# Linear attention feeding a two-layer network, on one core: tiles laid on 512-byte lines, w_in in three pieces, and a new order of one block's visits

## The chip, the core and the metric

The kernel runs on one core of one Trainium2 chip. The core has five engines that run side by side, each through its own list of instructions in order, and that wait for each other by semaphores: TensorE (PE, matmuls, with its weight loads shown as PEld), VectorE (DVE), ScalarE (ACT), GpSimd (POOL) and SyncE (SP, which here only issues transfers). Tiles lie in SBUF, 128 partitions wide; matmuls write to PSUM. Transfers from device memory are issued by SP, ACT or POOL and carried out by the core's 16 DMA engines. The metric is the time of one execution on the device in microseconds (us), the median over runs; lower is better.

## What is computed

q, k and v are fp32 of [4 batches, 8 heads, 768 positions, 64]. Each head keeps a state that decays, and its output is the input of a two-layer network with a leaky activation:

```python
gamma = 1.0 - 2.0 ** (-5.0 - np.arange(H, dtype=np.float32))
for t in range(S):
    state = gamma[None, :, None, None] * state + np.einsum('bhd,bhe->bhde', k[:, :, t], v[:, :, t])
    y[:, :, t] = scale * np.einsum('bhd,bhde->bhe', q[:, :, t], state)
...
x = np.ascontiguousarray(attn_out.transpose(0, 2, 1, 3)).reshape(B * S, H * D)
h = x @ w_in                                       # [3072, 512] @ [512, 2048]
g = np.maximum(h, 0.0) + alpha * np.minimum(h, 0.0)
return (g @ w_out).astype(np.float32)              # [3072, 2048] @ [2048, 512]
```

## The kernel before

**Tiling.** The 3072 tokens are 24 units of 128 positions, and six blocks of four units (512 tokens). Work on the attention goes by visits: visit i takes a pair of neighbouring units and half of the heads (four), so that block n has the visits 4n to 4n+3. The matmuls of the network go by blocks: `ffn1(n)` is 64 products of 128x512 (16 tiles of the 2048 hidden features, called ft, by four parts of the 512 inputs), `ffn2(n)` again 64 (four groups of 128 tokens by 16 ft).

**One visit.** `load` (L110) brings k, q and v of a visit, 256 KB each, as fp32, by SP. `u_scale(i, a)` (L128) multiplies k (a=0) or q (a=1) by powers of gamma and casts to f16, into the tile kdq; unless an engine is given, k goes to DVE and q to POOL. `u_cast` (L146) casts v to f16 (vx), on POOL or ACT. `u_turn` (L160) transposes kdq on PE (eight matmuls named trb), and ACT copies the result to SBUF (kq); later blocks use `u_flip`, a transposing transfer, instead. `u_state` (L183) sums k times v on PE (stp); the function that it returns, `advance`, adds this to the decayed state (DVE, ss, L218) and multiplies the sum with the next decay (POOL, tg, L219). At a sequence's first unit DVE does both at once (L214). `u_scores` (L225) multiplies q with k (sca, scb) and returns `masked`, with which DVE applies the mask (m, L249). `u_out` (L259) multiplies the scores with v and the queries with the decayed state (yps), and ACT copies that into xT, the network's input. `u_visit` (L533) is state, scores, decays and masks of one visit; `u_prep` (L540) is both scales and the cast.

**The network.** In `ffn1` each ft's product lands in a PSUM tile (hps); ACT takes relu(-h) (hm, L336) and DVE makes g from both (gt, L337). With early=4, the first four ft are computed on the block's first 256 tokens first, so that they can start before the second pair of units is out. In `ffn2` with parts=4 the 64 matmuls go in four groups of 16, each for four ft: the first 16 need the tiles 0 to 3 of w_out, the next 16 the tiles 4 to 7, and so on. ACT copies the results out (os).

**The order.** `manual_schedule` (L74) keeps the instructions of each engine in the order in which the kernel's lines name them. Both network functions are generators, and `tick(gen, m)` (L386) lets them emit m matmuls; between ticks the kernel names attention work of the next block. So in block 0's ffn2, the visits 4 to 7 of block 1 lie at stated distances. Since every engine goes in order, work named early on POOL stands ahead of work named later, whatever is ready.

**Weights.** w_in is fetched by POOL with a cast to f16 (`get_wi(lo, hi)`, L409, tiles lo to hi of 16), in four pieces of 2, 4, 4 and 6 tiles named among visits 1 to 3. `hold` (L415) lets the first load of w_out wait until the third piece (tiles 6 to 10) has landed. `load_wo(i)` (L426) fetches four tiles of w_out as fp32 by SP, in turn with the loads of visits 4 to 7, and `cast_wo` (L431) casts a tile to f16, on POOL or ACT. w_out's pieces and k, q, v share 24 buffers ("ld"). PSUM has eight tiles of 512 fp32, shared by everything ("ps", bufs=8). `keep(m)` (L97) is m matmuls on constant data.

**SBUF's layout.** The pools lay tiles one behind another. The first ones take per partition 208 bytes (tab), 768 (mi), 2048 (gmat), 512 (alpha), 1024 (spin), 4 (warm) and 64 (oma), each rounded up to 32 bytes, behind 16,512 bytes of other use; all that follow (w_in, w_out, the loads and the working tiles) take multiples of 512 and so begin 192 bytes past a multiple of 512.

Of the kernel before, what the change touches and what calls it, by code (L numbers as in the profile page):

```python
# [9 lines left out]
FP = mybir.dt.float32  # L10
F16 = mybir.dt.float16
# [7 lines left out]
def kernel(  # L19
# [13 lines left out]
    NFT = d_ff // 128  # L33
# [13 lines left out]
    NTAB = 4 * H + NP + 16  # L47
# [24 lines left out]
    sbp = ctx.enter_context(tc.tile_pool(name="sbp", bufs=1, space=bass.MemoryType.SB))  # L72
    psp = ctx.enter_context(tc.tile_pool(name="psp", bufs=1, space=bass.MemoryType.PSUM))
    ctx.enter_context(tc.manual_schedule())  # L74

    tab = sbp.tile([128, NTAB], FP, tag="tab", name="tab")
    mi = sbp.tile([128, 384], F16, tag="mi", name="mi")
    ident = mi[:, 0:128]
    masku = mi[:, 128:384].rearrange("p (s i) -> p s i", s=2)
    gmat = sbp.tile([128, NP, 128], FP, tag="gmat", name="gmat")  # L80
    alpha_sb = sbp.tile([NFT, 128], FP, tag="alpha", name="alpha")
    spin = sbp.tile([128, 512], F16, tag="spin", name="spin")
    warm = sbp.tile([128, 1], FP, tag="warm", name="warm")
    oma_sb = sbp.tile([128, NFT], FP, tag="oma", name="oma")
    w_in_all = sbp.tile([128, 4, d_ff], F16, tag="win", name="win")
    w_out_all = sbp.tile([128, NFT, d_model], F16, tag="wout", name="wout")

# [5 lines left out]
    def ps(name, dt=FP, n=512):  # L93
        return psp.tile([128, n], dt, tag="ps", bufs=8, name=name)


    def keep(m):  # L97
        pt = ps("kps")
        for i in range(m):
            nc.tensor.matmul(  # L100
                out=pt, lhsT=spin[:, 0:128], rhs=spin, start=True, stop=True
            )
# [5 lines left out]
    held = []  # L108
# [19 lines left out]
    def u_scale(i, a, eng=None):  # L128
        if i not in prepped:
            kdq = sbp.tile([128, 2, 2, H // 2, D], F16, tag="kdq", bufs=8, name=f"kdq{i}")  # L130
            kq = sbp.tile([128, 2 * NP, 128], F16, tag="kq", bufs=8, name=f"kq{i}")
            vx = sbp.tile([128, H // 2, 2, D], F16, tag="vx", bufs=8, name=f"vx{i}")
            prepped[i] = (kdq, kq, vx)
        g = i % 2
        o = 2 * H * a
        (eng or (nc.vector, nc.gpsimd)[a]).tensor_tensor(  # L136
            out=prepped[i][0][:, a],
            in0=staged[i]["kq"[a]].rearrange("p (h s d) -> p s h d", s=2, d=D),
            in1=tab[:, o : o + 2 * H]
            .rearrange("p (s h) -> p s h", s=2)[:, :, H // 2 * g : H // 2 * g + H // 2]  # L140
            .unsqueeze(3)
            .to_broadcast([128, 2, H // 2, D]),
            op=MULT,
        )

    def u_cast(i, on_scalar=False):  # L146
        o = prepped[i][2].rearrange("p h s d -> p (h s d)")
        x = staged[i]["v"]
        if on_scalar:
            nc.scalar.activation(out=o, in_=x, func=COPY, bias=0.0, scale=1.0)  # L150
        else:
            nc.gpsimd.tensor_copy(out=o, in_=x)  # L152
# [7 lines left out]
    def u_turn(i, parts):  # L160
        kdu, kq, vx = prepped[i]
        trb = ps("trb", F16, 1024)
        for a in parts:
            for x in range(NP):
                c0 = 128 * (NP * a + x)
                nc.tensor.transpose(  # L166
                    out=trb[:, c0 : c0 + 128],
                    in_=kdu[:, a, x // 2, 2 * (x % 2) : 2 * (x % 2) + 2, :].rearrange(
                        "p a d -> p (a d)"
                    ),  # L170
                    identity=ident,
                )
        c0 = 512 * parts[0]
        c1 = 512 * parts[-1] + 512
        nc.scalar.activation(  # L175
            out=kq.rearrange("p a i -> p (a i)")[:, c0:c1],
            in_=trb[:, c0:c1],
            func=COPY,
            bias=0.0,
            scale=1.0,  # L180
        )
# [77 lines left out]
    def u_out(i):  # L259
        j, g = divmod(i, 2)  # L260
        kqv, vx, m2s = live.pop(i)
        prepped.pop(i)
        ypss = [ps("yps"), ps("yps")]
        inter = [(2 * j + hf) % NCH > 0 for hf in range(2)]

        def carried(first):
            for hf in range(2):
                z = slice(64 * hf, 64 * hf + 64)
                for r in range(2):
                    if inter[hf]:  # L270
                        nc.tensor.matmul(  # L271
                            out=ypss[hf][:, 128 * r : 128 * r + 128],
                            lhsT=tgs[2 * j + hf][:, 2 * g + r, :],
                            rhs=kqv[:, 1, :, r, z],
                            start=(first and r == 0),
                            stop=(not first and r == 1),
                            skip_group_check=True,
                        )

        def own(first):  # L280
            for r in range(2):
                for s in range(2):
                    for lh in range(2):
                        for hf in range(2):
                            z = slice(64 * hf, 64 * hf + 64)
                            nc.tensor.matmul(  # L286
                                out=ypss[hf][64 * lh : 64 * lh + 64, 128 * r : 128 * r + 128],
                                lhsT=vx[z, 2 * r + lh, s, :],
                                rhs=m2s[lh][z, s, r, :],
                                start=(r == 0 and s == 0 and (first or not inter[hf])),  # L290
                                stop=(r == 1 and s == 1 and not (first and inter[hf])),
                                skip_group_check=True,
                            )

        if i < 2 * UB:
            own(True)
            carried(False)
        else:
            carried(True)
            own(False)  # L300
        n, jj = divmod(j, UB // 2)
        if n not in xT:
            xT[n] = sbp.tile([128, NP, TB], F16, tag="xT", bufs=2, name=f"xT{n}")
        for hf in range(2):
            c0 = C * (2 * jj + hf)
            nc.scalar.activation(  # L306
                out=xT[n][:, 2 * g : 2 * g + 2, c0 : c0 + C].rearrange(
                    "p a (i s) -> p a s i", s=2
                ),
                in_=ypss[hf][:, 0:256].rearrange("p (a s i) -> p a s i", a=2, s=2),  # L310
                func=COPY,
                bias=0.0,
                scale=1.0,
            )
# [71 lines left out]
    def tick(gen, m):  # L386
        for _ in range(m):
            if next(gen, 1) == 1:
                return
# [19 lines left out]
    def get_wi(lo, hi):  # L409
        s = slice(128 * lo, 128 * hi)  # L410
        return nc.gpsimd.dma_start(out=w_in_all[:, :, s], in_=wi[:, :, s])
# [19 lines left out]
    def cast_wo(ft, on_scalar=False):  # L431
        if on_scalar:
            nc.scalar.activation(
                out=w_out_all[:, ft, :], in_=pieces.pop(ft), func=COPY, bias=0.0, scale=1.0
            )
        else:
            nc.gpsimd.tensor_copy(out=w_out_all[:, ft, :], in_=pieces.pop(ft))  # L437

    m = {}
    st = {}  # L440
# [21 lines left out]
    st[0] = u_state(0)  # L462
    u_scale(2, 0)
    u_scale(2, 1)
    get_wi(0, 2)
    st[0](0)
    m[1] = u_scores(1)
    masked(1)
# [7 lines left out]
    st[1] = u_state(1)  # L476
    u_scale(3, 0)
    u_scale(3, 1)
    get_wi(2, 6)
    st[0](1)  # L480
    st[1](0)
    m[2] = u_scores(2)
    masked(2)
    keep(2)
    held.append(get_wi(6, 10))
    st[1](1)

    u_turn(3, (0, 1))
# [4 lines left out]
    st[2](0)  # L493
    get_wi(10, 16)
    m[3] = u_scores(3)
    keep(2)
    st[3] = u_state(3)
    m[3](0)
    st[3](0)
    m[3](1)  # L500
    for i in range(UB):
        load_wo(i)
        load(UB + i)
    gen = ffn1(0, early=4)
# [6 lines left out]
    nc.vector.tensor_scalar(  # L511
        out=oma_sb, in0=aps[:, 0:NFT], scalar1=-1.0, scalar2=1.0, op0=MULT, op1=ADD
    )
    st[2](1)
    st[3](1)
    for ft in range(4):
        cast_wo(ft)

    tick(gen, 8)
    u_out(3)  # L520
    tick(gen, 40)
    u_scale(4, 1)
    u_cast(4)
    for ft in range(4, 8):
        cast_wo(ft)
    tick(gen, 20)
    for _ in gen:
        pass
    u_scale(4, 0)
    stores = []  # L530
    gen = ffn2(0, parts=4, late=stores)

    def u_visit(i):  # L533
        st[i] = u_state(i)
        m[i] = u_scores(i)
        st[i](0)
        masked(i)
        st[i](1)

    def u_prep(i, eng=None):  # L540
        u_scale(i, 0, eng)
        u_scale(i, 1)
        u_cast(i)

    tick(gen, 6)
    u_turn(4, (0, 1))
    tick(gen, 6)
    u_visit(4)
    u_prep(5)
    tick(gen, 8)  # L550
    u_turn(5, (0, 1))
    tick(gen, 2)
    u_out(4)
    tick(gen, 4)
    u_visit(5)
    for ft in range(8, 12):
        cast_wo(ft, ft % 2)
    u_prep(6)
    tick(gen, 8)
    u_turn(6, (0, 1))  # L560
    tick(gen, 2)
    u_out(5)
    tick(gen, 4)
    u_visit(6)
    for ft in range(12, 16):
        cast_wo(ft, ft % 2)
    u_prep(7)
    tick(gen, 8)
    u_turn(7, (0, 1))
    tick(gen, 2)  # L570
    u_out(6)
    tick(gen, 4)
    u_visit(7)
    for _ in gen:
        pass
# [4 lines left out]
    gen = ffn1(1, early=4)  # L580
# [3 lines left out]
    for n in range(1, NBLK):  # L584
        more = n + 1 < NBLK
        u0 = UB * (n + 1)
        if n > 1:
            gen = ffn1(n)
# [9 lines left out]
        gen = ffn2(n)  # L598
# [41 lines left out]
```

## Time and profile before

| what | value |
|---|---|
| median of 3 runs | 224.21 us (224.03 to 225.7) |
| the profiled execution | 224.33 us, of which the profile's span is 222.5 us |
| granted TensorE clock in it | 0.997 |
| busy: PE, DVE, ACT, POOL | 208.7, 120.2, 102.7, 87.9 us |
| read from and written to device memory | 27.40 MB and 6.29 MB |
| share of the chain that ended last, PE and DMA | 75% and 10% |

The profile is one execution. A line of its timeline gives the start and the length in us, the engine, the line of the kernel, the operation, what it writes and reads (out<-in), the shape, a count, and in brackets how long the engine had been idle before it and which instruction ended that wait. Several instructions are merged in one line where nothing lies between them. Matmuls are pipelined: the length of one (0.22 to 0.38 us) is longer than the step from one to the next, and their ends are modelled.

### The profile page before, as it was taken

The numbers are of one execution on the slowest core, as the hardware profiler recorded it, in microseconds if no ns is written. First come the engines' busy times: TensorE is split into PE (matmuls) and PEld (weight loads), VectorE is DVE, ScalarE is ACT, GpSimd is POOL, SyncE is SP. The second block draws the span as 40 slices with busy tenths as digits, with TensorE's granted clock in tenths as the row PEclk, the third lists the DMA queues.
The fourth block names the chain that finished last, engine by engine and source line by source line (L and its number), as shares of the span: only waits on it lengthen the run. The fifth ranks groups of instructions, "written<-read, shape, count | busy, mean of one in ns | idle before, by whom it ended". The sixth has DMA issues, their size and how long they took to land.

```text
span 222.5 us, 5029 instructions
## 1 busy us (share of the span) xinstructions
PE 208.7 (94%) x2055; PEld 105.0 (47%) x2055; DVE 120.2 (54%) x195; ACT 102.7 (46%) x189; POOL 87.9 (39%) x115
## 2 busy tenths in 40 slices
PE   7898998875999999999999999999999999999992
PEld 3456544432564455444455444455444555444441
DVE  2773895434329852268935188645188652388000
ACT  2582862431657522366423377233476232676121
POOL 3486066465298041890023891111990231000000
PEclk9999999999999999999999999999999999999998
DMA  6999999999969971399911299911552012100111
GB/s 179 296 187 173 238 341 344 318 309 281 278 183 238 292 208 50 82 225 255 289 51 50 74 246 296 236 51 49 118 120 47 3 47 97 47 0 4 47 67 75
DMA packets 63127, 36.11 MB, mean 162 GB/s; under 512 B 18928, under 2 KB 57984, under 8 KB 63104
## 3 DMA queue, kind: packets, MB, share of 16 engines
q1 hardware_dynamic: 57792, 28.32, 50.9%
q10 hardware_dynamic: 3200, 5.38, 6.9%
q0 software_dynamic: 2112, 2.10, 6.2%
q8 instruction: 16, 0.26, 0.5%
q14 instruction: 7, 0.06, 0.1%
HBM read 27.40 MB, written 6.29 MB: 151 GB/s over the span
## 4 chain that ended last, share of the span: by engine, by line
PE 75%; DMA 10%; SPq 5%; POOL 4%; DVE 2%; issue 1%; ACT 1%; POOLq 0%; DVEq 0%
PE ops L367 35%; PE hps L326 31%; DMA win<-in_moe_w_in_dram 4%; DMA wo<-in_moe_w_out_dram 3%; SPq L118 3%; PE yps L286 3%; DMA qs<-in_q_dram 2%; PE stp L195 2%; PE yps L271 2%; SPq L429 2%; POOL wout L437 1%; PE sca L236 1%; POOL kdq L136 1%; DVE m L249 1%; POOL tg L219 1%
## 5 line engine op out<-in xcount | busy, mean ns | idle before, releaser
L337 DVE SCALAR_TENSOR_TENSOR gt<-hm,oma,hps 128x512 f16<-128x512 f32 x96 | 69.5, 745 | 37.2 <-ACT hm L336 29.9
L367 PE MATMUL ops<-wout,gt 128*128 128x512 f16 x384 | 89.3, 380 | 0.3 <-POOL wout L437 0.3
L326 PE MATMUL hps<-xT,win 128*128 128x512 f16 (+1 forms) x416 | 84.6, 363 | 1.2 <-DVE ss L218 0.9
L336 ACT ACTIVATE hm<-hps 128x512 f32<-128x512 f32 x96 | 56.5, 597 | 24.4 <-PE hps L326 22.7
L326 PEld LDWEIGHTS <-win 128*128 128x128 f16 x416 | 40.4, 98 | 43.5 <-DMA win<-in_moe_w_in_dram 1.0
L219 POOL TENSOR_TENSOR tg<-ss,gmat 128x256 f16<-128x256 f32 x32 | 23.5, 738 | 81.4 <-DVE ss L218 81.3
L367 PEld LDWEIGHTS <-gt 128*128 128x128 f16 x384 | 35.3, 98 | 40.7 <-issue 0.6
L306 ACT ACTIVATE xT<-yps 128x256 f16<-128x256 f32 x48 | 18.4, 453 | 34.8 <-PE yps L286 29.0
L376 ACT ACTIVATE os<-ops 128x512 f32<-128x512 f32 x24 | 14.3, 598 | 34.6 <-PE ops L367 34.6
L136 POOL TENSOR_TENSOR kdq<-qs,tab 128x512 f16<-128x512 f32 x24 | 25.1, 1046 | 6.3 <-DMA qs<-in_q_dram 6.3
L218 DVE TENSOR_TENSOR ss<-tg,stp 128x256 f32<-128x256 f16 x32 | 13.2, 415 | 25.8 <-PE stp L195 22.7
L175 ACT ACTIVATE kq<-trb 128x512 f16<-128x512 f16 (+1 forms) x11 | 8.7, 790 | 20.2 <-PE trb L166 20.2
L249 DVE TENSOR_TENSOR m<-sca,mi 128x512 f16<-128x512 f32 x24 | 16.4, 684 | 1.1 <-PE scb L236 0.7
L136 POOL TENSOR_TENSOR kdq<-ks,tab 128x512 f16<-128x512 f32 x16 | 16.8, 1047 | 0.0
L249 DVE TENSOR_TENSOR m<-scb,mi 128x512 f16<-128x512 f32 x24 | 16.3, 680 | 0.0
L152 POOL CAST vx<-vs 128x512 f16<-128x512 f32 x20 | 12.8, 638 | 0.0
L214 DVE TENSOR_TENSOR tg<-stp,gmat 128x256 f16<-128x256 f32 x8 | 3.4, 423 | 15.9 <-PE stp L195 15.8
L166 PE MATMUL trb<-mi,kdq 128*128 128x128 f16 x64 | 6.2, 227 | 6.0 <-POOL kdq L136 3.6
L437 POOL CAST wout<-wo 128x512 f16<-128x512 f32 x12 | 8.0, 678 | 9.3 <-DMA wo<-in_moe_w_out_dram 8.9
L195 PE MATMUL stp<-vx,kdq 64*64 64x128 f16 x320 | 9.7, 219 | 0.5 <-ACT vx L150 0.5
L286 PE MATMUL yps<-m,vx 64*64 64x128 f16 x384 | 10.0, 222 | 0.0
L236 PE MATMUL sca<-kq 64*64 64x128 f16 x192 | 9.5, 216 | 0.4 <-ACT kq L175 0.3
(26 smaller groups left out, 77.7 us busy)
## 6 DMA issues: line engine op xcount, KB each, us to landing
ks<-in_k_dram SPq DMA_DIRECT2D x24, 256.0 KB, 4.9
qs<-in_q_dram SPq DMA_DIRECT2D x24, 256.0 KB, 4.9
vs<-in_v_dram SPq DMA_DIRECT2D x24, 256.0 KB, 5.1
out_dram<-os ACTq DMA_DIRECT2D x20, 256.0 KB, 2.0
wo<-in_moe_w_out_dram SPq DMA_DIRECT2D x16, 256.0 KB, 5.8
win<-in_moe_w_in_dram POOLq DMA_DIRECT2D x2, 512.0 KB, 7.3
out_dram<-os SPq DMA_DIRECT2D x4, 256.0 KB, 2.7
win<-in_moe_w_in_dram POOLq DMA_DIRECT2D x1, 768.0 KB, 10.3
```

What stands on the lines that cost most here:

```text
L136: (eng or (nc.vector, nc.gpsimd)[a]).tensor_tensor(out=prepped[i][0][:, a], in0=staged[i]["kq"[a]].rearrange("p (h s d) -> p s h d", s=2, ...
L195: nc.tensor.matmul(out=stps[hf][64 * lh : 64 * lh + 64, 128 * r : 128 * r + 128], lhsT=kdu[z, 0, s, 2 * r + lh, :], rhs=vx[z, 2 * r : 2 * ...
L218: nc.vector.tensor_tensor(out=new, in0=tgs[u][:, gs, :], in1=stv, op=ADD)
L219: nc.gpsimd.tensor_tensor(out=tgs[u + 1][:, gs, :], in0=new, in1=gmat[:, gs, :], op=MULT)
L249: nc.vector.tensor_tensor(out=m2, in0=scs[lh].rearrange("p (s r i) -> p s r i", s=2, r=2), in1=masku.unsqueeze(2).to_broadcast([128, 2, 2, ...
L286: nc.tensor.matmul(out=ypss[hf][64 * lh : 64 * lh + 64, 128 * r : 128 * r + 128], lhsT=vx[z, 2 * r + lh, s, :], rhs=m2s[lh][z, s, r, :], s ...
L306: nc.scalar.activation(out=xT[n][:, 2 * g : 2 * g + 2, c0 : c0 + C].rearrange("p a (i s) -> p a s i", s=2), in_=ypss[hf][:, 0:256].rearran ...
L326: nc.tensor.matmul(out=hpss[ft][:, lo:hi], lhsT=w_in_all[:, hp, 128 * ft : 128 * ft + 128], rhs=xT[n][:, hp, lo:hi], start=(hp == 0), stop ...
L336: nc.scalar.activation(out=hm, in_=hpt, func=RELU, bias=0.0, scale=-1.0)
L337: nc.vector.scalar_tensor_tensor(out=gt[:, ft, :], in0=hm, scalar=oma_sb[:, ft : ft + 1], in1=hpt, op0=MULT, op1=ADD,)
L367: nc.tensor.matmul(out=opss[tq], lhsT=gt[:, ft, 128 * tq : 128 * tq + 128], rhs=w_out_all[:, ft, :], start=(ft == 0), stop=(ft == NFT - 1),)
L376: nc.scalar.activation(out=os_sb, in_=opss[tq], func=COPY, bias=0.0, scale=1.0)
```

## The change

Five things are changed. tab, mi, warm and oma are given larger tiles (384, 1024, 256 and 256 bytes per partition) of which the same part is used, so that the tiles behind them begin on multiples of 512 bytes. w_in is fetched in three pieces of 4, 6 and 6 tiles; the second is issued behind a decay of visit 0, and the loads of w_out wait for it. A keep(2) ahead of u_state(3) is gone, and the last decays of visits 2 and 3 (`st[2](1)`, `st[3](1)`) are named before ffn1(0). DVE's scale of k for visit 4 is named 12 matmuls ahead of ffn1's end (behind 13 of its 16 gt) and not after it. In ffn2(0), the turns, outs and casts of w_out are named at other places: u_out stands ahead of the next visit's turn, turn 5 stands 12 matmuls behind visit 4, and the scale and cast of visit 7 on POOL are named ahead of visit 6 and its decays.

```diff
-    tab = sbp.tile([128, NTAB], FP, tag="tab", name="tab")
-    mi = sbp.tile([128, 384], F16, tag="mi", name="mi")
+    tab = sbp.tile([128, 96], FP, tag="tab", name="tab")[:, 0:NTAB]
+    mi = sbp.tile([128, 512], F16, tag="mi", name="mi")[:, 0:384]
...
-    warm = sbp.tile([128, 1], FP, tag="warm", name="warm")
-    oma_sb = sbp.tile([128, NFT], FP, tag="oma", name="oma")
+    warm = sbp.tile([128, 64], FP, tag="warm", name="warm")[:, 0:1]
+    oma_sb = sbp.tile([128, 64], FP, tag="oma", name="oma")[:, 0:NFT]
...
-    get_wi(0, 2)
+    get_wi(0, 4)
     st[0](0)
...
     u_scale(3, 0)
     u_scale(3, 1)
-    get_wi(2, 6)
     st[0](1)
+    held.append(get_wi(4, 10))
     st[1](0)
     m[2] = u_scores(2)
     masked(2)
     keep(2)
-    held.append(get_wi(6, 10))
     st[1](1)
...
     get_wi(10, 16)
     m[3] = u_scores(3)
-    keep(2)
     st[3] = u_state(3)
     m[3](0)
     st[3](0)
+    st[2](1)
     m[3](1)
+    st[3](1)
...
-    st[2](1)
-    st[3](1)
+    tick(gen, 8)
+    u_out(3)
     for ft in range(4):
         cast_wo(ft)
-
-    tick(gen, 8)
-    u_out(3)
-    tick(gen, 40)
     u_scale(4, 1)
     u_cast(4)
     for ft in range(4, 8):
         cast_wo(ft)
-    tick(gen, 20)
+    tick(gen, 52)
+    u_scale(4, 0)
     for _ in gen:
         pass
-    u_scale(4, 0)
...
-    tick(gen, 6)
+    tick(gen, 4)
     u_turn(4, (0, 1))
     tick(gen, 6)
     u_visit(4)
     u_prep(5)
+    cast_wo(8)
+    cast_wo(10)
+    tick(gen, 10)
+    u_out(4)
+    tick(gen, 2)
+    u_turn(5, (0, 1))
+    cast_wo(9, True)
+    cast_wo(11, True)
+    tick(gen, 6)
+    u_visit(5)
+    u_prep(6)
+    cast_wo(12)
+    cast_wo(14)
     tick(gen, 8)
-    u_turn(5, (0, 1))
+    u_out(5)
     tick(gen, 2)
-    u_out(4)
-    tick(gen, 4)
-    u_visit(5)
-    for ft in range(8, 12):
-        cast_wo(ft, ft % 2)
-    u_prep(6)
+    u_turn(6, (0, 1))
+    cast_wo(13, True)
+    cast_wo(15, True)
+    u_scale(7, 1)
+    u_cast(7)
+    tick(gen, 6)
+    u_visit(6)
+    u_scale(7, 0)
     tick(gen, 8)
-    u_turn(6, (0, 1))
+    u_out(6)
     tick(gen, 2)
-    u_out(5)
-    tick(gen, 4)
-    u_visit(6)
-    for ft in range(12, 16):
-        cast_wo(ft, ft % 2)
-    u_prep(7)
-    tick(gen, 8)
     u_turn(7, (0, 1))
-    tick(gen, 2)
-    u_out(6)
-    tick(gen, 4)
+    tick(gen, 6)
     u_visit(7)
```

## The prediction

> **What bounds the kernel now.** The page first: TensorE (PE) is busy for 94% of the span, so only places where PE idles, or is released late, can give time back.
>
> ```profile
> span 222.5 us, 5029 instructions
> PE 208.7 (94%) x2055; PEld 105.0 (47%) x2055; DVE 120.2 (54%) x195; ACT 102.7 (46%) x189; POOL 87.9 (39%) x115
> ```
>
> Next, the table by stretch, cut where PE changes stage: prologue with visits 0 to 3 (0 to 16.86), ffn1 of block 0 (to 33.33), ffn2 of block 0 with block 1's visits 4 to 7 (to 60.80), ffn1 of block 1 (to 75.41), the rest. Columns: us of the stretch, then busy us of each engine.
>
> ```profile
> 0.00:16.86 16.86, 14.25 (x219) 7.29 (x219) 9.63 (x18) 9.32 (x17) 9.59 (x17) 1.00 0.97 221
> 16.86:33.33 16.47, 15.58 (x128) 8.78 (x123) 11.55 (x20) 10.17 (x19) 7.03 (x11) 1.00 1.11 250
> 33.33:60.80 27.47, 21.37 (x267) 10.38 (x266) 11.79 (x20) 10.43 (x18) 13.80 (x19) 1.00 1.07 305
> 60.80:75.41 14.61, 14.30 (x98) 8.02 (x97) 9.53 (x14) 9.79 (x18) 10.71 (x13) 1.00 0.97 233
> 75.41:222.50 147.09, 143.20 (x1355) 70.54 (x1352) 77.68 (x125) 62.98 (x118) 46.73 (x58) 1.00 0.44 112
> ```
>
> From 60.80 on PE is full. The third stretch loses 6.1 us of 27.47. Its PE timeline (start, us, what, idle before and releaser) says where:
>
> ```profile
> 35.70 0.62 PE L166 MATMUL trb<-mi,kdq 128*128 128x128 f16 x8 [0.92 <-DVE kdq L136]
> 40.90 0.62 PE L166 MATMUL trb<-mi,kdq 128*128 128x128 f16 x8 [0.89 <-DVE kdq L136]
> 45.78 0.59 PE L367 MATMUL ops<-wout,gt 128*128 128x512 f16 x2 [0.32 <-POOL wout L437]
> 47.81 0.40 PE L166 MATMUL trb<-mi,kdq 128*128 128x128 f16 x4 [1.08 <-POOL kdq L136]
> 53.17 0.40 PE L166 MATMUL trb<-mi,kdq 128*128 128x128 f16 x4 [0.59 <-DVE kdq L136]
> 55.87 0.40 PE L166 MATMUL trb<-mi,kdq 128*128 128x128 f16 x4 [2.30 <-POOL kdq L136]
> ```
>
> Every large wait is a transpose (u_turn) waiting for a scaled kdq. The POOL timeline tells why the two on GpSimd are late: the scale stands behind a decay (tg), which waits for the previous visit, and behind two casts of w_out.
>
> ```profile
> 52.69 1.01 POOL L219 TENSOR_TENSOR tg<-ss,gmat 128x256 f16<-128x256 f32 x1 [4.38 <-DVE ss L218]
> 53.65 1.16 POOL L437 CAST wout<-wo 128x512 f16<-128x512 f32 x2
> 54.78 1.03 POOL L136 TENSOR_TENSOR kdq<-qs,tab 128x512 f16<-128x512 f32 x1
> ```
>
> In the second stretch PE's one idle place is at 18.74 to 19.63; the timeline of weight loads says that it waits for w_in's second piece (issued 13.74, landing 5.8 later by the DMA view, 19.6):
>
> ```profile
> 19.62 0.77 PEld L326 LDWEIGHTS <-win 128*128 128x128 f16 x8 [0.98 <-DMA win<-in_moe_w_in_dram]
> ```
>
> **The change part by part.** Sums are against the profiled execution: span 222.5, time 224.33, 0.1 above the median of 224.21.
>
> *Block 1's visits.* A 128x512 matmul of the dense stretches takes 0.216 us (64 in 13.81 on the chain). PE's true idle, from the end of the matmuls issued before: 33.33+6x0.216=34.63 to 35.70 is 1.07; 38.11+8x0.216=39.84 to 40.90 is 1.06; 43.99+1.30=45.29 to 45.78 is 0.49; 46.56 (four transposes, 0.23) to 47.81 is 1.25; 52.41 to 53.17 is 0.76; 53.40 to 55.87 is 2.47. Together 7.1. The work itself is the same 64 matmuls, four turns and visits and three outs: 27.47-7.1=20.4. Now each wait under the new order, T being the start of ffn2(0), 33.3 before.
> Turn 4 (T+0.86, two matmuls earlier): DVE scales k4 after 13 of the 16 gt instead of after all. The 16 ran back to back from 23.14 (0.735 each), so kdq starts at 32.7 and takes 0.69 to 0.82: 33.5, before 34.2. The three gt behind it end 0.8 later, 35.7; the scores that reuse their PSUM are issued at 35.9 or later. GpSimd's kdq4 ended at 33.3. Cost nothing, cover 0.2 to 0.9.
> Turn 5 stood 8 matmuls behind visit 4; it now has 12 and u_out(4), 12x0.216+0.57=3.2. DVE needs 0.43 to ss, then ss 0.4, two m 1.2, kdq 0.7 to 1.24: 2.7 to 3.3 from the end of visit 4. Just covered.
> Turns 6 and 7 have 10 matmuls and u_out (2.7) behind the visit; GpSimd needs, from the visit's end, ss at 0.85, tg 0.7, kdq 1.0: 2.6 for turn 6; casts 12 and 14 and vx come behind. For turn 7, kdq7 and vx7 stand ahead of the decays of visits 6 and 7, so nothing of visit 6 holds them; DVE's kdq7 comes after m, m and ss as for turn 5, so 0 to 0.3 may stay. What waits behind: the decays of visits 6 and 7, whose readers are block 2's visits, over 15 us later; nothing.
> Casts: 8 and 10 stand behind prep 5, two each go to ACT behind turn 5 and turn 6, so matmul 33 (five behind visit 5) finds them; what can stop them is the landing.
> Landings: w_out 7 lands at 29.77+7.60=37.4 and is cast by 38.0; matmul 20, its first reader, comes at about T+5.3, 38.6. w_out 11 (35.3 plus up to 7.5) lands 42.8; ACT casts it by 43.4, its first reader is matmul 36 at about T+10.4, 43.7. q7 (43.64+6.1) lands 49.8, kdq7 by 50.8; turn 7 is wanted at T+17.1=50.4. So if nothing lands earlier, 0.4 remains. I take 7.0 of the 7.1 back, between 6.4 and 7.1.
>
> *w_in in 4, 6, 6.* The first piece is twice as large and is issued at the same place (11.02); ft 2 and 3 no longer wait for a piece issued at 13.74. From rows: the 512 KB pieces took 5.8 alone and 8.75 queued; the 256 KB one 5.7 beside the last k, q, v loads. So it lands between 16.9 and 18.3; 16.7 plus the added 256 KB at 205 GB/s (1.3), less the gap of about 0.8 in which the old first piece was drained by laggards, 17.2 to 17.5. PE wants it at 16.86 (waits 0.5) and saves the 0.89 at 18.74: -0.4, between -0.9 and +0.6. ft 4 now lies in piece two, wanted at 21.19+8x0.216-0.4=22.5. Its issue moves behind one decay on POOL (14.5, against 13.74 and 15.24 for the two pieces it replaces); the bytes up to its end are the same 1.25 MB as for the old third piece, which landed at 24.0 and was wanted at 24.6. Ends: 24.0 as before, and 17.4 plus 768 KB at 205 GB/s, 21.2. I take the middle, 22.7, and a wait of 0.2, of 0 to 1.5. The w_out loads held behind it start 0 to 2.8 earlier, on SP, where nothing else is queued. The two decays that stood around the issues move under 0.8, within DVE's own waits. Piece three, issued 0.7 earlier, is wanted at 28, landed at 27.7 before.
>
> *Removed keep(2)* (two matmuls, 0.43): stp(3) waits for vx3, cast by ACT until 16.43, so PE idles there instead. Nothing. st[2](1), st[3](1) earlier and their decays: DVE 0.8 before the m of unit 3's second half, which ends 18.5; PE needs it for u_out(3) at 19.4. Nothing.
>
> *512-byte lines.* By the tiles' sizes every loaded tile began 192 bytes past a multiple of 512, and now begins on one. No row shows an aligned load. Below: nothing. Above: the loads' rate against the best in the trace, k/q/v at 295 GB/s (5 to 13 us), w_out's 2 KB rows 380, w_in read in fp32 at twice 205:
>
> ```profile
> DMA packets 4744, 2.36 MB, mean 295 GB/s; under 512 B 141, under 2 KB 4744, under 8 KB 4744
> ```
> ```profile
> DMA packets 301, 0.31 MB, mean 205 GB/s; under 512 B 0, under 2 KB 301, under 8 KB 301
> ```
>
> So a 256 KB load takes between 0.89 and 0.64. That reading goes at 410 while the loads, read from the same HBM, stay at 295 speaks for a limit on the load's own packets, which alignment may touch; I take 0.72. Then q3 (landed 12.67) comes 1.6 earlier, but DVE is nearly full from 7.8 to 14.7, so ffn1(0) comes about 0.5 earlier, w_in's issue 1.0 earlier; and the 0.1 to 0.4 left at turns 6 and 7 goes. -0.6, between 0 and -1.5. A loss is excluded: no tile becomes less aligned. After 60.80 loads are hidden: nothing.
> [...]
>
> Sum: 224.33-7.0-0.4+0.2-0.6=216.5; less 0.1 to the median: 216.4.
>
> **The rivals.** *Alignment does nothing* (for: the rate may be set by packet count, 512 bytes each; against: the 410 above): the -0.6 goes and 0.3 of waits stays: 217.3.
> *The load stream becomes the bound of the visits.* DMA's share is over 0.97 of 16 engines through 60.80. PE asks for wo and q7 seven us earlier; one landing in this stretch (w_out 7: 7.6 from its issue, its neighbours about 6) came 1.5 us beyond their pace. One such on q7 puts 1.5 back, 217.9; another on w_out 11 some 0.9 more: 218.8.
> *w_in's second piece is late* and with it PE and all w_out loads, for the hold is on it. If it takes 10.3 like the slowest piece, it lands at 24.8: 2.0 lost: 218.5.
> *Other side: the same, to the point of no gain.* It needs piece two at 22.7+7.9=30.6, 16 us after issue. No piece took over 10.3. Time then 224.5 and more.
> *VectorE against GpSimd.* The DVE kdq at 39.61 took 1.24 beside a GpSimd kdq (0.69 alone), and four kdq now meet casts. 4x0.55=2.2 on engines with idle time; on PE at most 0.5 at turns 5 and 7: 216.9. It lies inside the forecast.
>
> **How the numbers follow.** Forecast 0.45 (own range 215.2 to 217.0), alignment nothing 0.33, load stream 0.10, late piece 0.07, no gain or worse 0.05. A measurement of this kernel tells about 1% (2.2 us) from no change. All but the last lie below 222.0: faster 0.93, same 0.04, slower 0.03. The range takes in the first four and is opened below to 214.9 by the rest of alignment's -1.5 and of the first piece's -0.9: 214.9 to 219.0.
>
> **What would show it.** Right: ffn2(0) starts near 32.7 and the next ffn1 about 20.5 later; no wait on kdq over 0.4 at the turns; the first hps waits about 0.5 for w_in, the second not; k/q/v at over 340 GB/s. Wrong: turns still waiting for kdq; PE waiting for w_in at ft 4 by over 1 us; stretches after that not 32.2 us per block as before.

## The result, and the profile after

| kernel | median us (runs) | ratio to the kernel before, 95% interval |
|---|---|---|
| before, beside it | 224.95 (4) | |
| changed | 217.0 (4, 216.47 to 220.59) | 0.9628 [0.9538, 0.9717] |
| changed, in a later set | 217.47 (6, 216.3 to 220.39) | 0.9635 [0.9588, 0.9682] |

The change makes the kernel 3.7% faster, and 216.4 was forecast. Medians here and below are over all runs, ratios leave disturbed ones out, so the two can stand a little apart. The profiled execution took 217.12 us at a granted clock of 0.998, with a span of 215.3. Against the profiled execution of before (224.33) that is 7.2 us, or 3.2%. The rest up to 3.7% can lie in the clock: of the 30 runs of the kernel before that were made beside the experiments with more than one run, 24 had a mean granted clock of 0.992 or less and took 225.4 us or more, the other six had 0.997 or more and took 224.1 to 224.8. Of the ten runs of the changed kernel eight had 0.997 or more. At that clock the means are 224.5 and 217.1 us, a gain of 3.3%.

The page of the changed kernel, first the sums by engine:

```profile
span 215.3 us, 5025 instructions
PE 207.2 (96%) x2053; PEld 105.4 (49%) x2053; DVE 120.6 (56%) x195; ACT 102.9 (48%) x189; POOL 87.0 (40%) x114
```

PE's busy time fell by 1.5 us and the span by 7.2: what went is mostly idle time. The table by stretch, cut at the same places of the work as that of before (prologue; ffn1 of block 0; ffn2 of block 0 with block 1's visits; ffn1 of block 1; the rest):

```profile
0.00:16.86 16.86, 13.80 (x216) 7.46 (x216) 9.67 (x18) 9.27 (x17) 9.86 (x17) 1.00 0.93 233
16.86:33.45 16.59, 15.67 (x121) 8.77 (x122) 11.79 (x20) 10.18 (x19) 8.41 (x13) 1.00 1.10 292
33.45:53.66 20.21, 20.21 (x267) 10.67 (x266) 10.79 (x19) 10.54 (x18) 11.07 (x15) 1.00 1.11 352
53.66:68.27 14.61, 14.30 (x98) 8.02 (x97) 10.49 (x17) 9.78 (x18) 10.96 (x13) 1.00 0.90 242
68.27:215.30 147.03, 143.20 (x1355) 70.51 (x1352) 77.88 (x125) 63.10 (x118) 46.72 (x58) 1.00 0.43 114
```

The third stretch went from 27.47 to 20.21, and PE is now busy in all of it with the same 267 instructions. The two stretches ahead of it together got 0.12 longer (33.33 to 33.45), the last two stayed (161.70 and 161.64). -7.26+0.12-0.06 is -7.2. The PE timeline of the third stretch has the four turns and the start of the next ffn1, none with an idle time in brackets:

```profile
34.31 0.61 PE L166 MATMUL trb<-mi,kdq 128*128 128x128 f16 x8
39.99 0.61 PE L166 MATMUL trb<-mi,kdq 128*128 128x128 f16 x8
45.24 0.61 PE L166 MATMUL trb<-mi,kdq 128*128 128x128 f16 x8
50.38 0.61 PE L166 MATMUL trb<-mi,kdq 128*128 128x128 f16 x8
53.66 1.04 PE L326 MATMUL hps<-xT,win 128*128 128x256 f16 x8
```

The POOL timeline shows why turn 7, which waited 2.30 before, no longer does: its scale and cast (46.69, 47.67) are done before the decay (tg) that waits for visit 6.

```profile
46.69 1.04 POOL L136 TENSOR_TENSOR kdq<-qs,tab 128x512 f16<-128x512 f32 x1
47.67 0.60 POOL L152 CAST vx<-vs 128x512 f16<-128x512 f32 x1
49.66 1.02 POOL L219 TENSOR_TENSOR tg<-ss,gmat 128x256 f16<-128x256 f32 x1 [1.38 <-PE ops L367]
```

The opening, where a gain of 0.8 was forecast and none came, in the PE timeline from the first matmul of ffn1(0) to ffn2(0):

```profile
17.42 1.05 PE L326 MATMUL hps<-xT,win 128*128 128x256 f16 x8 [0.56 <-DMA win<-in_moe_w_in_dram]
19.24 0.28 PE L326 MATMUL hps<-xT,win 128*128 128x256 f16 x1
19.88 0.92 PE L326 MATMUL hps<-xT,win 128*128 128x256 f16 x7 [0.36 <-ACT xT L306]
...
33.45 1.03 PE L367 MATMUL ops<-wout,gt 128*128 128x512 f16 x4
```

Two waits are new. The first is for the larger piece of w_in, as forecast (0.5). The second is not in the forecast: u_out(2) has just been issued, which writes columns 256 to 511 of the first two input parts of xT, and the next matmuls read columns 0 to 255. The one on the first input part goes, and the next, on the second input part, waits for ACT's copy all the same.

### The profile page after: what moved, and what is told of

The parts are those of the page before. It is cut to its first block, busy times and chain, and to the rows that moved or that the text cites. A ratio compares the mean times of both kernels' runs of the same rounds, so it can differ in the third digit from the quotient of the medians.

```text
span 215.3 us, 5025 instructions
## 1 busy us (share of the span) xinstructions
PE 207.2 (96%) x2053; PEld 105.4 (49%) x2053; DVE 120.6 (56%) x195; ACT 102.9 (48%) x189; POOL 87.0 (40%) x114
## 3 DMA queue, kind: packets, MB, share of 16 engines
q1 hardware_dynamic: 57792, 28.32, 48.5%
HBM read 27.40 MB, written 6.29 MB: 156 GB/s over the span
## 4 chain that ended last, share of the span: by engine, by line
PE 89%; DMA 6%; SPq 2%; ACT 1%; POOL 0%; issue 0%
PE ops L367 40%; PE hps L326 39%; PE yps L286 4%; DMA win<-in_moe_w_in_dram 3%; DMA qs<-in_q_dram 3%; PE stp L195 2%; PE yps L271 2%; PE sca L236 2%; SPq L118 2%; PE trb L166 1%; ACT xT L306 1%; PE scb L236 1%; POOL kdq L136 0%; ACT os L376 0%
## 5 line engine op out<-in xcount | busy, mean ns | idle before, releaser
L437 POOL CAST wout<-wo 128x512 f16<-128x512 f32 x12 | 7.5, 651 | 7.0 <-DMA wo<-in_moe_w_out_dram 6.9
L236 PE MATMUL scb<-kq 64*64 64x128 f16 x192 | 9.7, 219 | 0.0
```

Source lines behind the costliest of these rows:

```text
L236: nc.tensor.matmul(out=scs[lh][z, c0 : c0 + 128], lhsT=kqv[y, 0, s, r, z], rhs=kqv[y, 1, :, r, z], start=True, stop=True,)
```

## The experiments

Theory 1: the gain is the order of block 1's visits alone. Theory 2: the loads on aligned lines give a part or all of it. A third question is what the pieces of w_in do.

**The old order, with all else changed** (everything that the change moves from u_out(3) to visit 7 undone; two places of it):

```diff
-    tick(gen, 52)
-    u_scale(4, 0)
+    tick(gen, 20)
     for _ in gen:
         pass
+    u_scale(4, 0)
...
-    u_scale(7, 1)
-    u_cast(7)
-    tick(gen, 6)
+    tick(gen, 4)
     u_visit(6)
-    u_scale(7, 0)
+    for ft in range(12, 16):
+        cast_wo(ft, ft % 2)
+    u_prep(7)
```

> The changed kernel with block 1's visits (turns, outs, scales, casts of w_out, and the scale of visit 4) in the old order; the new layout and the pieces of 4, 6, 6 stay. Theory 1 (the order on GpSimd and VectorE made the waits): the six waits of the third stretch come back, ffn2(0) lasts 27 us again, less at most 1 for earlier loads; span 221 to 222.5, ratio to before about 0.995. Theory 2 (the waits were for late loads, which the layout and the pieces now bring earlier): most of the gain stays, span under 219.

225.05 us (median of 10 runs), ratio 0.9933 [0.9895, 0.997]. The PE timeline of its third stretch has all six waits of before again, though the loads are fast:

```profile
38.45 0.62 PE L166 MATMUL trb<-mi,kdq 128*128 128x128 f16 x8 [0.78 <-DVE kdq L136]
43.65 0.62 PE L166 MATMUL trb<-mi,kdq 128*128 128x128 f16 x8 [0.89 <-DVE kdq L136]
48.53 0.59 PE L367 MATMUL ops<-wout,gt 128*128 128x512 f16 x2 [0.32 <-POOL wout L437]
50.56 0.40 PE L166 MATMUL trb<-mi,kdq 128*128 128x128 f16 x4 [1.08 <-POOL kdq L136]
55.92 0.40 PE L166 MATMUL trb<-mi,kdq 128*128 128x128 f16 x4 [0.60 <-DVE kdq L136]
58.62 0.40 PE L166 MATMUL trb<-mi,kdq 128*128 128x128 f16 x4 [2.30 <-POOL kdq L136]
```

The stretch is 27.33 long (36.22 to 63.55). So these waits are of the order on the engines, not of late transfers.

**The old tiles, with all else changed** (`tab`, `mi`, `warm` and `oma` at their old sizes).

> The changed kernel with tab, mi, warm and oma in their old sizes, so that all tiles begin 192 bytes past a multiple of 512 again. Theory 1: loads of k, q, v take 0.88 us each again and not 0.76; the visits' order covers it but for 0.3 to 0.6 us; span 215.5 to 216.2, ratio to before 0.965 to 0.97. Theory 2: the visits wait for loads again, above all turn 7 for q7; span over 217.5. If alignment does nothing to loads they stay at 0.76 and the span at 215.3.

217.25 us (4 runs), ratio 0.9634 [0.9586, 0.9682]: the same as the changed kernel. The loads took 0.89 us each again (table below), and the third stretch is 20.21 as well, without waits.

**The new tiles alone in the kernel before.**

> The kernel before with the new sizes of tab, mi, warm and oma alone. Theory 1: loads of k, q, v go from 0.88 to 0.76 us each, yet the turns go on waiting behind the casts and decays: span 221.5 to 222.5, ratio 0.995 to 1. Theory 2: the waits for kdq shrink with the loads, span under 220.

226.65 us over 10 runs, ratio 0.995 [0.9905, 0.9995]. In its profile the six waits stand as before, and ffn2(0) starts at 32.83, 0.5 earlier. Half a per cent in the kernel before, nothing in the changed one: theory 2 falls as a cause of the 3.7%.

**The old pieces of w_in, with all else changed.**

```diff
-    get_wi(0, 4)
+    get_wi(0, 2)
...
+    get_wi(2, 6)
     st[0](1)
-    held.append(get_wi(4, 10))
     st[1](0)
...
     keep(2)
+    held.append(get_wi(6, 10))
     st[1](1)
```

> The changed kernel with w_in in its old four pieces of 2, 4, 4, 6 at their old places. In the changed kernel PE waits 0.56 for the first piece and then 0.5 for a copy of xT that the old wait for the second piece had covered. Theory 1 (the pieces gained next to nothing): span within 0.4 of 215.3. Rival (the third piece is again what w_out waits for, and comes 1 to 2 us later, so visit 4's reads of w_out wait): span over 216.3. My forecast had put the pieces at a gain of 0.2.

216.79 us (4 runs, 216.45 to 221.63), ratio 0.9604 [0.9547, 0.9662]; the profiled span is 214.9 and ffn2(0) starts at 32.88. The first piece (256 KB) lands at 15.13 and PE waits 0.19 for the second. The difference to the changed kernel is inside the intervals; the new pieces are not shown to give anything.

**One wait put back at a time.** In the first kernel the scale of q and the cast of visit 7 come behind visit 6 on POOL; in the second, DVE's scale for visit 4 comes behind all 16 gt:

```diff
-    u_scale(7, 1)
-    u_cast(7)
     tick(gen, 6)
     u_visit(6)
     u_scale(7, 0)
+    u_scale(7, 1)
+    u_cast(7)
```

> The changed kernel with the scale and cast of visit 7 on GpSimd named behind visit 6 and not ahead of it, so behind its decay again. Theory 1 (the order on GpSimd made the wait): from visit 6's end ss of the second unit ends at about 1.9, tg at 2.7, kdq at 3.7 us, and turn 7 is wanted 2.7 behind: a wait on GpSimd's kdq of 1.0 at turn 7, span 216.3. If the distance of 10 matmuls and the out were enough by themselves: no wait, 215.3.

```diff
-    u_scale(4, 0)
     for _ in gen:
         pass
+    u_scale(4, 0)
```

> The changed kernel with VectorE's scale of k for visit 4 named behind all 16 gt again. In the changed kernel 13 gt end at 32.35 and kdq at 33.1; the last three take 2.05. Then kdq ends at 35.2 and turn 4, wanted at 34.3, waits 0.8 to 0.9 on VectorE's kdq: span 216.1. If the early scale gained nothing: 215.3.

The PE timelines (first the one with visit 7, then the one with visit 4):

```profile
54.77 0.40 PE L166 MATMUL trb<-mi,kdq 128*128 128x128 f16 x4 [0.96 <-POOL kdq L136]
```
```profile
35.00 0.62 PE L166 MATMUL trb<-mi,kdq 128*128 128x128 f16 x8 [1.21 <-DVE kdq L136]
```

The third stretches are 21.35 and 21.60 long, 1.14 and 1.39 more than 20.21. Each wait comes back alone, and costs about its idle time. At turn 7 that is 0.96 of the 2.30 before; there the two casts of w_out (1.16 us) stood between the decay and the scale as well, and here they don't. The other four waits were put back together only, with the old order. The times are 221.3 and 217.82, one run each. The former's other 3 us lie in the opening: its first piece of w_in landed only at 19.34, though nothing of the edit stands ahead of it.

**Where the line lies.** Every loaded tile moved 64 bytes past a multiple of 512 (`warm` of 80 floats, not 64), and 256 bytes past one (128 floats).

> The changed kernel with 64 bytes more ahead of w_in, so that all loaded tiles begin 64 bytes past a multiple of 512. Loads of k, q, v take 0.757 us each at 0 and 0.877 at 192. If any run that crosses a 512-byte line pays the same: 0.87. [...] Span within 0.4 of 215.3 in both.

> The changed kernel with 256 bytes more ahead of w_in, so that all loaded tiles begin 256 bytes past a multiple of 512. If lines of 512 bytes matter: loads of 0.87 us as at 192. [...] Span within 0.4 of 215.3 in both.

218.3 and 216.46 us, one run each. The spans, 216.5 and 214.7, miss the expected 215.3 by more than 0.4: PE waited 1.02 us for the first piece of w_in in the one, and hardly in the other. In the prologue nine 256 KB loads land one behind another between k of visit 1 and v of visit 3. By the landings of the DMA view, one takes:

| tiles lie past a multiple of 512 by | kernel | us per 256 KB |
|---|---|---|
| 192 bytes | before | (14.50-6.33)/9 = 0.91 |
| 192 bytes | changed, old tiles | (14.72-6.75)/9 = 0.89 |
| 64 bytes | changed | (15.06-7.02)/9 = 0.89 |
| 256 bytes | changed | (13.48-6.54)/9 = 0.77 |
| 0 | changed | (13.75-6.92)/9 = 0.76 |

The nine other profiles with tiles on a multiple of 512 give 0.76 to 0.78. No trace shows a tile's address; the differences between the offsets come from the tiles' sizes, their zero from the 16,512 bytes ahead of the first tile, which no trace shows either. The times fall into two groups by these offsets. So a multiple of 512 is not needed: at 256 the loads took 0.77, as at 0, and both offsets tried off a multiple of 256 cost the same, 0.89 to 0.91. An offset of 128 was not tried. What was moved is the side that the loads write.

**The false wait taken out.** For the third and fourth early ft, the matmuls with the input part that waits for ACT's copy go last (`last` names the input part that ends the sum):

```diff
-        def product(ft, lo, hi, hps=range(4)):
+        def product(ft, lo, hi, hps=range(4), last=3):
...
-                    stop=(hp == 3),
+                    stop=(hp == last),
...
+        late_hp = 1 if n == 0 else 3
         for ft in range(early):
             hpss[ft] = ps("hps")
-            yield from product(ft, 0, TB // 2)
+            if ft < 2:
+                yield from product(ft, 0, TB // 2)
+            else:
+                some = [hp for hp in range(4) if hp != late_hp]
+                yield from product(ft, 0, TB // 2, some, late_hp)
+        for ft in range(2, early):
+            yield from product(ft, 0, TB // 2, [late_hp], late_hp)
```

> The changed kernel, pieces of 4, 6, 6, with ffn1's early tiles in the other order alone. Theory: 0.7 to 1.0 below the changed kernel on the same chip. If the wait on xT is not what the second half of the first tiles waits for: no difference.

216.65 us (6 runs, 215.71 to 218.64), ratio 0.9614 [0.9562, 0.9666]. Its PE timeline:

```profile
18.28 1.05 PE L326 MATMUL hps<-xT,win 128*128 128x256 f16 x8 [1.18 <-DMA win<-in_moe_w_in_dram]
...
20.09 1.05 PE L326 MATMUL hps<-xT,win 128*128 128x256 f16 x8
...
33.78 1.03 PE L374 MATMUL ops<-wout,gt 128*128 128x512 f16 x4
```

The wait on xT is gone: ffn1(0) takes 33.78-18.28=15.50 from its first matmul, 33.45-17.42=16.03 in the changed kernel. What it saves here, 0.53, went to the first piece of w_in, which landed at 18.23. By the kernel's lines the waiting matmul reads other columns than the copy writes. These lie between the two parts that ACT writes (columns 256 to 511 and 768 to 1023 of the tile; the matmul reads 512 to 767). So a wait for the whole stretch that the copy spans fits, and one for the data does not; no run tests this further. The gain in time, 216.65 against 217.47 in the same set, is inside the intervals.

**The changed kernel again, and a first piece of 6 tiles** (`get_wi(0, 6)`, then tiles 6 to 10).

> The changed kernel again, to be held against the others on the same chip. Its first piece of w_in landed at 17.4 in its profile; in the runs that share it, issued at about the same place, it landed between 16.6 and 19.3. Theory: the times scatter by up to 3 us with this landing, the long ones with a lower granted clock behind the wait; 216.4 to 217.5 for most.

> The changed kernel with a first piece of 6 tiles (6, 4, 6), to take the late landing further. Theory: it lands 1.2 us later than that of 4 tiles, at 18 to 20, PE waits 1.5 to 3 us for it, and the granted clock halves for some 3.4 us behind waits of about 1.9 and more, as in the two runs where that piece landed at 19.1 and 19.3: span 217 to 220. Rival: the landing depends on the loads beside it and not on its size: span within 0.5 of the changed kernel.

217.47 us (6 runs) and 219.7 (4 runs, 217.29 to 221.93). In the first profile, of the same kernel as the one above, the first piece landed at 16.09 and PE did not wait for it:

```profile
16.57 1.05 PE L326 MATMUL hps<-xT,win 128*128 128x256 f16 x8
...
18.39 0.28 PE L326 MATMUL hps<-xT,win 128*128 128x256 f16 x1
19.03 0.93 PE L326 MATMUL hps<-xT,win 128*128 128x256 f16 x7 [0.36 <-ACT xT L306]
...
32.60 1.03 PE L367 MATMUL ops<-wout,gt 128*128 128x512 f16 x4
```

ffn2(0) starts at 32.60 and not 33.45: two executions of one kernel differ here by as much as the opening was forecast to gain. With 6 tiles the piece landed at 17.91 and PE waited 1.59. Its 7.4 us from issue to landing lie within what the smaller piece took in other profiles (5.6 to 8.2), so that the size makes it late is not shown. The table by stretch (PEclk is the third column from the right) shows that this costs more than the wait:

```profile
18.00:19.00 1.00, 1.00 (x12) 0.72 (x16) 0.16 (x1) 0.00 (x0) 1.00 (x2) 0.97 1.26 210
19.00:20.00 1.00, 1.00 (x21) 0.68 (x20) 0.00 (x0) 0.06 (x1) 0.08 (x1) 0.50 1.23 218
20.00:21.00 1.00, 0.91 (x6) 0.49 (x5) 0.17 (x1) 0.70 (x2) 0.00 (x0) 0.50 1.14 204
21.00:22.00 1.00, 1.00 (x7) 0.68 (x5) 0.00 (x0) 0.00 (x0) 0.00 (x0) 0.50 1.17 212
22.00:23.00 1.00, 1.00 (x23) 0.58 (x22) 0.00 (x0) 0.00 (x0) 0.00 (x0) 0.82 1.15 216
```

After the wait the clock is half for some 3.4 us (from 18.94 to 22.35 by the trace; the means of 0.97 and 0.82 give the same to 0.02), and ffn1(0) takes 35.05-17.96=17.09. In the two other profiles where PE waited long for this piece, 1.87 us (the old order) and 2.37 (visit 7 late), it takes 17.10 each, at half clock as well; after waits of 0.56, 1.02 and 1.18 the clock stayed at 1. That a wait of 1.59 was enough was not expected ("about 1.9 and more").

The length of the wait alone doesn't decide. The 2.30 us ahead of turn 7 in the kernel before left the clock at 1.00 (third stretch of the prediction's table), and so did the same 2.30 with the new tiles alone (mean clock 0.999) and with the old order (0.990, which beside the 3.42 at half clock in its opening leaves about 1.1 us at half clock for all the rest). In five traces the clock keeps a value for 3.41 us or a multiple of that: half for 3.41, 3.40 and 3.42 us in the three profiles (to 0.02), full for 215.04 us (63 times 3.413, from 6.29 to 221.33) in the trace of the kernel before and for 208.21 us (61 times, from 6.46 to 214.67) in that of the changed one. In the three profiles with half clock, PE was idle for 2.0 to 2.3 us of the 3.41 just ahead of the fall (about 0.4+1.59, 0.4+1.87, and 2.28 of the 2.37). If steps of 3.41 us are counted on from the changes of each trace, an estimate where the clock doesn't change, each of the three waits of 2.30 fell across two steps, with at most 1.8 us idle in either (0.51 and 1.79 in the kernel before). So idle time within one step fits all these cases; that the clock goes by it is the author's estimate, which no run tests by itself. By it a wait of 2.30 can also fall into one step whole. That this is why most runs of the kernel before had a lower mean clock is not shown: the one trace of that kernel is at 0.997.

**All that looked good at once:** the false wait taken out, and the old pieces of w_in.

> The changed kernel with w_in in the old pieces of 2, 4, 4, 6, and with ffn1's early tiles in another order: of ft 2 and 3, the matmul that waits for ACT's copy into xT (hp 1 in block 0, hp 3 in block 1, whose columns the wait covers though the copy writes others) comes after the six that do not. The pieces alone gave a span of 214.9. Theory: the waits of 0.36 and 0.31 us go, with about as much behind them: span 214.0 to 214.4, ratio to before 0.955 to 0.958. Rival: the next wait (the u_out behind them, or the landing of w_in at ft 4) takes them over: 214.7 and more.

219.79 us (6 runs: two at 216.4 and 216.5 with a mean clock of 1.0, four at 219.6 to 220.3 with 0.989 to 0.992), ratio 0.9643 [0.9564, 0.9722]. The profile is one of the two:

```profile
16.77 1.05 PE L326 MATMUL hps<-xT,win 128*128 128x256 f16 x8
...
19.37 1.05 PE L326 MATMUL hps<-xT,win 128*128 128x256 f16 x8 [0.72 <-DMA win<-in_moe_w_in_dram]
...
33.06 1.03 PE L374 MATMUL ops<-wout,gt 128*128 128x512 f16 x4
```

The second piece landed at 19.32 and stopped PE in the place of the first, so the rival came true. Nothing here is shown to beat the changed kernel.

## Why the prediction was right, and which terms were not

The mechanism that carries the sum held, and the number is near for that reason; the small terms were off. In the profiled pair the opening, forecast at -0.8 in all, gave +0.12. That the sum missed by only 0.6 us (216.5 against 217.12) is helped by 0.26 more than forecast from the visits.

*Block 1's visits, -7.0.* Right in mechanism and size: 7.26 came back, theory 1 stands by the old order (27.33) and by the single waits put back. The 0.1 to 0.4 that it left at turn 7 isn't there. It reckoned with q7 landing at 49.8, with loads starting as before. They start when piece two of w_in has landed (22.17, before 24.01), q7 itself is issued 4.2 earlier (39.45, before 43.64), and it landed at 44.67. With the old tiles q7 landed at 47.80 and the stretch is 20.21 too, so this doesn't need the faster loads.

*VectorE against GpSimd.* The cause came, the price didn't: DVE's kdq took 1.24 us twice (four were feared), at 38.21 and 43.89, and no turn waited for it.

*w_in in 4, 6, 6, -0.4 and +0.2: mis-sized.* The landing (17.2 to 17.5 forecast, 17.37 measured) and its wait (0.5, measured 0.56) held. What failed is "saves the 0.89 at 18.74". Under that wait lay another, for ACT's copy of xT, which showed once it was gone: ffn1(0) from its first matmul went from 33.33-16.86=16.47 to 16.03, a saving of 0.44. So 0.56-0.44 is +0.12, not -0.4. In the second profile of the changed kernel, where PE did not wait for the piece, ffn2(0) starts 0.73 earlier than before: this term's sign is a matter of one execution. Piece two landed at 22.15 and cost nothing (+0.2 forecast).

*512-byte lines, -0.6: mis-sized.* The loads did get faster (0.91 to 0.76 us, 0.72 taken), so the rival's reason, a rate set by the count of packets, is wrong (57,792 packets on the queue of the loads in both profiles). But its time of 217.3 is nearer to the 217.0 and 217.5 measured than the forecast is, because the faster loads gave next to nothing. In the profiled run the chain began late (k of visit 1 at 6.92, before 6.33) and q of visit 2 landed at 9.97 as before (9.96), so w_in was issued at 11.02 as before; PE was ready for ffn1(0) at 17.42-0.56=16.86, as before. In the second profile of the changed kernel it was ready at 16.57, with w_in issued at 10.51: 0.3 us earlier, where 0.5 was forecast. Against the changed kernel with the old tiles, ready at 17.48-0.20=17.28, the two are 0.4 and 0.7 earlier; but the first piece landed at 17.43 there and at 17.37 in the first of them, so PE spent the gain waiting for it. With k of visit 1 landing anywhere from 6.26 to 7.33 in these profiles, such differences between single executions are not sure.

*What was missing* is the spread of the first piece's landing. For 512 KB it landed 5.6 to 8.2 us after its issue in nine profiles, at 16.1 to 19.3 us, where the forecast had "between 16.9 and 18.3"; 256 KB took 4.1 to 5.7. Later than about 16.8, each us is lost, and in the three profiles with waits of 1.59 and more the half clock took another 1.1 (17.1 against 16.03). The forecast has no term for the clock. Why one execution's piece takes 2 us more than another's isn't settled; nothing in the profiles tells it apart from chance on the queues.

## What to carry to other kernels

When an engine's list is in order, put work whose input is there ahead of work that waits for another engine, and check waits by putting them back: six idle times of 0.5 to 2.5 us went so, 7.26 us in all, and two of them, put back alone, came back. Before a wait is counted as saved, look for the one that lies under it. A transfer that a full engine waits for wants a margin as large as the spread of its landing (here 5.6 to 8.2 us after its issue for 512 KB), which one profile doesn't show.

## What the runs showed of the hardware

Loads into SBUF tiles that by the tiles' sizes begin 0 or 256 bytes past a multiple of 512 took 0.76 to 0.78 us per 256 KB in rows of 512 bytes, at 64 and 192 bytes 0.89 to 0.91. TensorE's clock fell to half after waits of 1.59, 1.87 and 2.37 us in the opening, each with 2.0 to 2.3 us of idle time in the 3.41 us just ahead of the fall, and came back 3.40 to 3.42 us later; it stayed full after waits of 0.56, 1.02 and 1.18 us there, and after three of 2.30 that by the author's estimate were split between two steps of 3.41.
